# Retention, low-rank mixer and two feed-forwards on one core: the head of a token block is fetched back from DRAM when its turn comes

## The chip, the cores and the metric

The kernel runs on one core of one Trainium2 chip. The metric is device time in microseconds (us) of one execution; less is better. Engines are named as in the profile: PE (TensorE matmuls), PEld (TensorE weight loads), DVE (VectorE), ACT (ScalarE), POOL (GpSimd), and SP, whose queue (SPq) issues every DMA of this kernel in the order in which they are written.

## The reference

Three layers on 8 sequences of 576 tokens, model width 512:

```
ret = (scale * q k^T) * Dmat            # decaying causal weights, 8 heads of 64
x   = ret @ v                           # [8, 576, 512]
u   = x + (x^T U V)^T                   # rank 32, over the 576 tokens of a sequence
x2  = u + relu(u @ w_ch1) @ w_ch2       # 512 -> 2048 -> 512
k   = relu(mix_k(x2) @ w_k); v = (k*k) @ w_v
out = sigmoid(mix_r(x2) @ w_r) * v      # mix: each token with the one before it
```

Everything is fp32; a product is made of three fp32r matmuls from a high and a low part of each operand (high x high, low weight x high, high weight x low).

## The kernel before

The 4608 tokens are cut in two ways that do not fit each other: 8 batches (sequences) of S = 576 and 9 blocks of BT = 512. Block b consists of the last 64b columns of batch b-1 and the first 512-64b columns of batch b. I call the former the **head** of block b.

**The first stage** runs over 40 steps, five to a batch (`step_of`, i = 5b+p). A step does the retention of 128 tokens of its batch (lines 839 to 967: `scores`, `decay`, `inter`, `own`, `gain`, `states`, `leave`), and between those PE is filled with `hidden(n)`: n of the 16 products of block b-1 with `w_ch1` (12 matmuls each, line 383; ACT applies the ReLU out of one of two PSUM banks, line 389, and SP stores the result, line 394). So while batch b is in its five steps, PE works off the hidden products of block b-1. After the last step of batch b come `low_rank_sum` (two steps later) and `later` (three steps later), which puts eight `mix` matmuls and then `mix_store(b)` on the list `todo`; one entry of it is taken after each third of a hidden product.

**mix_store(b)** writes batch b's u to DRAM (`u_blk[b]` and the head of `u_blk[b+1]`), splits its first columns into the high and low parts of block b, and splits the rest at once into the head of block b+1. The parts of a block are four SBUF units (`ublk[t]`: `uh` x2, `ul` x2, [128, 2, 512] each). The block's hidden products read them through the whole of the next batch, so from `mix_store(b)` on, eight units are held: four of block b in use, and four of block b+1 with only the head in them.

**The pool.** All of this is in the pool `big`, 35 units of 4 KB per partition, one tag. A unit goes to the next tile in the program's order and its new writer waits by a semaphore for the last reader of the old tile. Besides `ublk` and 16 units of resident `w_ch1`, `big` holds the q/k/v loads (`qk`, `kv`, loaded four steps ahead) and, between the hidden products, the **weight conversions**: `slot()` takes a weight that is stored as float64 through a raw load (`wkraw`, `wv_raw`, `wsraw`, `wrraw`), ACT's word arithmetic (lines 100, 104), DVE's join (107), ACT's cast of a high part (lines 132, 270, 314) and POOL's or DVE's low part (lines 133, 271, 315), and stores it to DRAM (`keys`, `gates`, `second`, `wv_kept`, `first`). The order of every engine is the order written here (a manual schedule); nothing overtakes.

After the first stage (to about 546 us) come the pair of last blocks in seven products (line 1342), the down projection (line 557), and the gates, keys and values (lines 1429, 1525).

Of the kernel before, what the change touches and what calls it, by code (L numbers as in the profile page):

```python
# [9 lines left out]
F32 = mybir.dt.float32  # L10
F32R = mybir.dt.float32r
# [5 lines left out]
ALU = mybir.AluOpType  # L17
PSUM = bass.MemoryType.PSUM

B, H, S, D = 8, 8, 576, 64  # L20
# [10 lines left out]
L = 64  # L31
# [7 lines left out]
PAIR = (NB - 2, NB - 1)  # L39
# [4 lines left out]
def retention_mixer_kernel(ctx: ExitStack, tc: tile.TileContext, io):  # L44
    nc = tc.nc

    consts = ctx.enter_context(tc.tile_pool(name="consts", bufs=1))
    big = ctx.enter_context(tc.tile_pool(name="big", bufs=35))
# [3 lines left out]
    u_blk = [dram.tile([128, KD, BT], F32, name=f"ub{t}") for t in range(NB)]  # L52
# [7 lines left out]
    def unit(pool, dt, nm):  # L60
        return pool.tile([128, 2, 512], dt, tag="unit", name=nm)
# [6 lines left out]
    def bank(n, nm):  # L68
        return psum[-1].tile([128, 512], F32, tag=f"b{n}", name=nm, bufs=1)
# [4 lines left out]
    def turn(kind, banks, nm):  # L74
        i = turns.get(kind, 0)
        turns[kind] = i + 1
        return bank(banks[i % len(banks)], nm)
# [211 lines left out]
    def first_sums(g):  # L289
        got = {}  # L290

        def whole():
            got["x"] = [cv.tile([128, 512], F32, tag="cf", name="cf", bufs=5) for _ in range(2)]
            for i, x in enumerate(got["x"]):
                f = g + HF * i
                w, c = w1[f // 4], slice((f % 4) * 128, (f % 4 + 1) * 128)
                for k in range(2):
                    nc.vector.tensor_tensor(
                        x[:, 256 * k:256 * k + 256].rearrange("p (k n) -> p k n", n=128),
                        w.h[k][:, :, c].bitcast(F32), w.l[k][:, :, c].bitcast(F32), op=ALU.add,  # L300
                    )

        def sums():
            x, y = got["x"]
            a11, a12, a21, a22 = x[:, :256], x[:, 256:], y[:, :256], y[:, 256:]
            nc.vector.tensor_tensor(a22, a21, a22, op=ALU.add)
            nc.vector.tensor_tensor(a21, a11, a21, op=ALU.subtract)
            nc.vector.tensor_tensor(a11, a22, a11, op=ALU.subtract)
            nc.vector.tensor_tensor(a12, a12, a11, op=ALU.subtract)

        def part(i):
            x = got["x"][1 - i]
            y = got[i] = unit(big, F32R, f"fs{g}_{i}")
            nc.scalar.copy(y[:, 0], x)  # L314
            nc.vector.tensor_tensor(y[:, 1], x, y[:, 0].bitcast(F32), op=ALU.subtract)  # L315

        def store(i):
            nc.sync.dma_start(
                kept_1[g][:, i], got[i].bitcast(F32).rearrange("p l (s n) -> p l s n", n=256)
            )  # L320

        return [whole, sums, lambda: part(0), lambda: store(0), lambda: part(1), lambda: store(1)]
# [35 lines left out]
    ublk = {}  # L358


    def split_u(t, c0, x, n):
        if t not in ublk:
            ublk[t] = (
                [unit(big, F32R, f"uh{t}_{j}") for j in range(2)],
                [unit(big, F32R, f"ul{t}_{j}") for j in range(2)],
            )
        h, l = ublk[t]
        for j in range(2):
            hj, xj = h[j][:, :, c0:c0 + n], x[:, 2 * j:2 * j + 2]
            nc.scalar.copy(hj, xj)  # L370
            nc.vector.tensor_tensor(l[j][:, :, c0:c0 + n], xj, hj.bitcast(F32), op=ALU.subtract)
# [398 lines left out]
    with ExitStack() as st:  # L770
# [27 lines left out]
        def scale_k(b, p):  # L798
            n = 2 if p < NC - 1 else 1
            k = kv[b, p][:, :n, :256].rearrange("p c (h d) -> p c h d", d=D)  # L800
            nc.gpsimd.tensor_tensor(k, k, ktab[:, p, :n].to_broadcast([128, n, NP, D]), op=ALU.mult)  # L801
# [223 lines left out]
        def mix(b, k, s):  # L1025
            o, n = SEG[s]
            ps = turn("m", ("n", 0, 1), f"mx{b}_{k}_{s}") if b == 0 else bank("n", f"mx{b}_{k}_{s}")
            nc.tensor.matmul(  # L1028
                ps[:, :n], gst[b][:, k * 128:(k + 1) * 128], vst[:, o:o + n], start=True, stop=True
            )  # L1030
            u = xt[b][:, k, o:o + n]
            nc.vector.tensor_tensor(u, ps[:, :n], u, op=ALU.add)  # L1032

        def mix_store(b):
            o = (b + 1) * BT - b * S
            u = xt.pop(b)
            if b < PAIR[0]:
                split_u(b, BT - o, u[:, :, :o], o)
            if b + 1 < PAIR[0]:
                split_u(b + 1, 0, u[:, :, o:], S - o)  # L1040
            nc.sync.dma_start(u_blk[b][:, :, BT - o:], u[:, :, :o])
            nc.sync.dma_start(u_blk[b + 1][:, :, :S - o], u[:, :, o:])
            if b < PAIR[0]:
                ready.extend((b, f) for f in range(NF))
            if b + 1 == PAIR[0]:
                for j in range(2):
                    even.append(unit(big, F32, f"ue{j}"))
                    nc.sync.dma_start(even[j][:, :, :S - o], u_blk[b + 1][:, 2 * j:2 * j + 2, :S - o])
            if b == PAIR[0]:
                for j in range(2):  # L1050
                    nc.gpsimd.tensor_copy(even[j][:, :, BT - o:], u[:, 2 * j:2 * j + 2, :o])
                    odd.append(u[:, 2 * j:2 * j + 2, o:])


        todo, ready = [], []
        even, odd = [], []

        def mixes(n):
            for _ in range(n):
                if todo:  # L1060
                    todo.pop(0)()

        def later(b):
            for k in range(KD):
                for s in range(2):
                    todo.append(lambda k=k, s=s: mix(b, k, s))
            todo.append(lambda: mix_store(b))

        def hidden(n, convert=True):
# [75 lines left out]
        def stages(i):  # L1145
            for stage in early.pop(i, []):
                stage()
# [22 lines left out]
        for g in range(HF):  # L1170
            x = first_sums(g)
            if sums:
                before, begin = sums[-1], x[0]
                sums[-1] = lambda before=before, begin=begin: (before(), begin())
                x = x[1:]
            sums.extend(x)

        def load_to(n):
            while units and N - len(units) < n:
                load(*units.pop(0))  # L1180
# [17 lines left out]
        def next_qtab(p):  # L1198
            for a in range(NP):
                nc.scalar.activation(  # L1200
                    qtab[:, p, a], qtab[:, p - 1, a], AF.Copy, scale=step[:, a, 0:1]
                )
# [5 lines left out]
        def plan(i, fn, *args, where=due):  # L1208
            where.setdefault(i, []).append((fn, args))
# [3 lines left out]
        def products_of(i):  # L1213
            inter(i)
            own(i)
            if i + 1 < N:
                scores(i + 1)
                gain(i + 1)

        def leaves_of(i):  # L1220
            if i + 1 < N:
                decay(i + 1)
            from_state(i)
            if i + 1 < N:
                states(i + 1)
            leave(i)

        def step_of(i):
            b, p = seq[i]
            load_to(i + 4)  # L1230
            if i + 2 < N:
                scale_k(*seq[i + 2])
            for fn, args in first.pop(i, []):
                fn(*args)
            products_of(i)
            if i == NC:
                mixes(9)
            leaves_of(i)
            last = p == NC - 1
            if last and b == 0:  # L1240
                plan(i, natural, b, p)
                plan(i + 1, low_rank, b, p, where=first)
                plan(i + 1, low_rank_sum, b, where=first)
                plan(i + 1, later, b, where=first)
            else:
                plan(i + 1, natural, b, p)
                plan(i + (1 if i == NC - 2 else 2), low_rank, b, p)
                if last:
                    plan(i + 2, low_rank_sum, b)
                    plan(i + 3, later, b)  # L1250
            if i < NC - 1:
                next_qtab(i + 1)
            for fn, args in due.pop(i, []):
                fn(*args)
            if not ready:
                mixes(9)
            n = FIRST[i - NC] if i < len(FIRST) + NC else FULL[p] if b < B - 1 else LAST[p]
            for x in range(2):
                if b:
                    hidden((n + 1 - x) // 2, False)  # L1260
                if i or x:
                    stages(2 * i + x)
                if i > 2 * NC + 2 and not todo:
                    quiet.append(i)
                    slot(new=len(quiet) % 2 == 1 or len(quiet) > 40)
                    if sums:
                        sums.pop(0)()

        for i in range(N):
            step_of(i)  # L1270
# [12 lines left out]
        while ready:  # L1283
            if len(ready) == 3:
                load_first(0)
            t, f = ready.pop(0)
# [393 lines left out]
```

## Time and profile before

| | |
|---|---|
| median of 3 runs | 1443.59 us (1439.63 to 1444.34) |
| the profiled execution | 1441.68 us, span of its instructions 1439.9 us |
| TensorE clock granted, mean of the span | 0.970 |
| PE / DVE / ACT / POOL busy | 94% / 64% / 47% / 26% of the span |

A granted clock of 1.00 is 2.4 GHz, its other level, 0.5, is 1.2 GHz; a stretch in which both occur shows a mean between. Times in the trace count from the first instruction.

### The profile page before, as it was taken

How to read it: one execution, taken by the hardware profiler on the slowest of the kernel's cores; microseconds unless marked ns; L12 is line 12 of the kernel's file. 1: busy time of each engine (PE TensorE's matmuls, PEld its weight loads, DVE VectorE, ACT ScalarE, POOL GpSimd, SP SyncE). 2: the span in 40 equal slices, each digit the busy share in tenths (PEclk: the TensorE clock that was granted, in tenths of full speed). 3: DMA queues.
4: the chain of work that ended last, by engine and by line, in shares of the span. 5: the costliest groups of instructions: out<-in, count | busy, mean ns of one | idle time of the engine just before them, and what ended most of it. 6: DMA issues, size and time to landing. Idle time of an engine off the chain costs nothing.

```text
span 1439.9 us, 26131 instructions
## 1 busy us (share of the span) xinstructions
PE 1350.4 (94%) x10248; PEld 1103.1 (77%) x10248; DVE 915.8 (64%) x1268; ACT 677.3 (47%) x1185; POOL 379.8 (26%) x317
## 2 busy tenths in 40 slices
PE   7899885788869989999999999999999999999998
PEld 5688674667657778778888888888888888888897
DVE  3644442455335243577979798788797797687753
ACT  4654433244344345654444444466455455565431
POOL 2341232243415101402222121220411402303312
PEclk8899998999989999999999999999999999999999
DMA  9667586689849628799978888589238157075272
GB/s 346 223 228 256 196 301 222 216 289 313 296 158 357 236 107 263 263 372 408 323 255 287 278 281 278 206 294 342 96 147 284 38 214 254 1 254 184 72 279 89
DMA packets 134827, 342.11 MB, mean 238 GB/s; under 512 B 16432, under 2 KB 29616, under 8 KB 134704
## 3 DMA queue, kind: packets, MB, share of 16 engines
q1 hardware_dynamic: 134704, 340.44, 67.2%
q8 instruction: 81, 1.33, 0.4%
q14 instruction: 42, 0.34, 0.1%
HBM read 232.38 MB, written 108.00 MB: 236 GB/s over the span
## 4 chain that ended last, share of the span: by engine, by line
PE 70%; DMA 5%; DVE 4%; ACT 2%; issue 2%; SPq 1%; POOL 1%; DVEq 0%; ACTq 0%; POOLq 0%
PE v L1525 13%; PE h L383 11%; PE gc L557 6%; PE ga L557 6%; PE gd L557 6%; PE kd L1429 3%; PE kc L1429 3%; PE ka L1429 3%; PE gb L557 3%; PE kb L1429 2%; PE rd L1429 2%; PE rc L1429 2%; PE ra L1429 2%; PE c L639 1%; PE c L638 1%
## 5 line engine op out<-in xcount | busy, mean ns | idle before, releaser
L389 ACT ACTIVATE hs<-h 128x512 f32<-128x512 f32 x112 | 65.8, 596 | 155.0 <-PE h L383 153.3
L1481 POOL TENSOR_TENSOR vl<-m,vh 128x512 fp32r<-128x512 f32 (+1 forms) x40 | 47.7, 1193 | 310.2 <-ACT vh L1480 238.8
L516 ACT CAST sbh<-rb 128x1024 fp32r<-128x1024 f32 x64 | 67.3, 1052 | 52.0 <-PE gd L557 41.0
L1525 PE MATMUL v<-vh,wv_0u 128*128 128x512 f32 x288 | 88.7, 389 | 0.0
L1525 PE MATMUL v<-vh,wv_1u 128*128 128x512 f32 x288 | 88.7, 389 | 0.0
L517 DVE TENSOR_TENSOR sbl<-rb,sbh 128x1024 fp32r<-128x1024 f32 x64 | 84.3, 1317 | 3.4 <-ACT sbh L516 3.3
L516 ACT CAST sah<-ra 128x1024 fp32r<-128x1024 f32 (+1 forms) x64 | 53.5, 837 | 57.7 <-DVE ra L498 29.4
L517 DVE TENSOR_TENSOR sal<-ra,sah 128x1024 fp32r<-128x1024 f32 (+1 forms) x64 | 66.6, 1040 | 20.3 <-PE gd L557 12.2
L315 DVE TENSOR_TENSOR fs<-cf,fs 128x512 fp32r<-128x512 f32 x16 | 12.3, 767 | 103.3 <-ACT fs L314 92.2
L1481 POOL TENSOR_TENSOR vl<-c,vh 128x512 fp32r<-128x512 f32 (+1 forms) x40 | 62.2, 1575 | 25.8 <-ACT vh L1480 25.8
L1032 DVE TENSOR_TENSOR xt<-mx,xt 128x256 f32<-128x256 f32 x64 | 28.7, 456 | 56.8 <-PE mx L1028 56.7
L1525 PEld LDWEIGHTS v<-vh,wv_1u 128*128 128x128 f32 x288 | 54.1, 188 | 11.2
L1525 PEld LDWEIGHTS v<-vh,wv_0u 128*128 128x128 f32 x288 | 53.9, 188 | 11.0
L383 PE MATMUL h<-uh,w_2h 128*128 128x512 f32 x112 | 35.2, 440 | 27.9 <-ACT hs L389 27.9
L1480 ACT CAST vh<-m 128x512 fp32r<-128x512 f32 (+1 forms) x40 | 23.2, 580 | 75.3 <-DVE m L1479 75.3
L801 POOL TENSOR_TENSOR kv<-kv,ktab 128x512 f32<-128x512 f32 (+1 forms) x40 | 40.7, 1018 | 63.8 <-DMA kv<-in_kv 57.6
L1525 PE MATMUL v<-vl,wv_0u 128*128 128x512 f32 x144 | 56.0, 389 | 0.0
L1525 PE MATMUL v<-vl,wv_1u 128*128 128x512 f32 x144 | 56.0, 389 | 0.0
L601 POOL TENSOR_TENSOR x<-x,ur 128x512 f32<-128x512 f32 x16 | 25.1, 1581 | 105.7 <-DVE x L597 101.7
L670 ACT ACTIVATE tp<-x2l,omu 128x511 f32<-128x511 f32 x72 | 50.9, 712 | 3.1 <-DMA x2l<-xb 3.1
L853 DVE TENSOR_TENSOR pm<-up,dtab 128x512 f32<-128x512 f32 (+1 forms) x40 | 25.3, 632 | 41.1 <-PE up L839 41.1
L574 POOL TENSOR_TENSOR m<-m,ur 128x512 f32<-128x512 f32 x8 | 12.3, 1559 | 139.2 <-ACT m L571 139.2
(375 smaller groups left out, 3999.3 us busy)
## 6 DMA issues: line engine op xcount, KB each, us to landing
wk<-keys SPq DMA_DIRECT2D x80, 512.0 KB, 6.0
rb<-hp SPq DMA_DIRECT2D x64, 512.0 KB, 6.5
hp<-hs SPq DMA_DIRECT2D x112, 256.0 KB, 3.8
wr<-gates SPq DMA_DIRECT2D x40, 512.0 KB, 6.1
qk<-in_qk SPq DMA_DIRECT2D x32, 512.0 KB, 6.0
kv<-in_kv SPq DMA_DIRECT2D x32, 512.0 KB, 6.3
ra<-hp SPq DMA_DIRECT2D x32, 512.0 KB, 7.1
ur<-ub SPq DMA_DIRECT2D x18, 512.0 KB, 6.4
```

The lines of the kernel that those rows point to most:

```text
L383: nc.tensor.matmul(hps[t, f], w.part(lo, k, fo), u[k // 2][:, k % 2, :], start=(part == 0 and k == 0), stop=(part == 2 and k == KD - 1),)
L389: nc.scalar.activation(h, hps.pop((t, f)), AF.Relu)
L516: nc.scalar.copy(hi_, src)
L517: nc.vector.tensor_tensor(lo_, src, hi_.bitcast(F32), op=ALU.subtract)
L557: nc.tensor.matmul(group[g][p], l[:, col(p)], r, start=(h == 0 and j == 0 and i == 0), stop=(i == 2 and last), skip_group_check=True,)
L670: nc.scalar.activation(tp[:, 1:], x[:, :BT - 1], AF.Copy, scale=omu[:, j, k:k + 1])
L801: nc.gpsimd.tensor_tensor(k, k, ktab[:, p, :n].to_broadcast([128, n, NP, D]), op=ALU.mult)
L853: nc.vector.tensor_tensor(m[:, :, :n], t[:, :, 0:n * 128].rearrange("p g (x i) -> p g x i", i=2 * L), dtab.to_broadcast([128, 2, n, 2 * L] ...
L1032: nc.vector.tensor_tensor(u, ps[:, :n], u, op=ALU.add)
L1429: nc.tensor.matmul(ps[b], l, r[:, i], start=(part == 0 and i == 0 and j == 0), stop=(i == 1 and j == 2), skip_group_check=True,)
L1481: eng.tensor_tensor(l, x, h.bitcast(F32), op=ALU.subtract)
L1525: nc.tensor.matmul(vacc[t][o], w.part(lo, g, col(o)), x[:, i, :], start=(g == 0 and i == 0 and j == 0), stop=(g == NG - 1 and i == 1 and j ...
```

## The change

`mix_store(b)` no longer splits the head of block b+1 (but for b = 0). In its place `fetch_head(b)`, two steps after batch b's last one, allocates two units `uf` and loads block b's head from `u_blk[b]` by two DMAs; `split_head(b)`, put on `todo` just ahead of `mix_store(b)`, allocates the four units of `ublk[b]` and splits the head into them (ACT copy, DVE subtract). It is done for b = 2 to 6. The two `mixes(9)` become `mixes(10)`, since the list has one entry more.

```
+        def fetch_head(b):
+            heads[b] = [unit(big, F32, f"uf{b}_{j}") for j in range(2)]
+            for j, x in enumerate(heads[b]):
+                nc.sync.dma_start(x[:, :, :L * b], u_blk[b][:, 2 * j:2 * j + 2, :L * b])
+
+        def split_head(b):
+            ublk[b] = tuple([unit(big, F32R, f"u{x}{b}_{j}") for j in range(2)] for x in "hl")
+            for j, x in enumerate(heads.pop(b)):
+                hj, xj = ublk[b][0][j][:, :, :L * b], x[:, :, :L * b]
+                nc.scalar.copy(hj, xj)
+                nc.vector.tensor_tensor(ublk[b][1][j][:, :, :L * b], xj, hj.bitcast(F32), op=ALU.subtract)
...
         def mix_store(b):
...
-            if b + 1 < PAIR[0]:
-                split_u(b + 1, 0, u[:, :, o:], S - o)
+            if b == 0:
+                split_u(1, 0, u[:, :, o:], S - o)
...
+            if 1 < b < PAIR[0]:
+                todo.append(lambda: split_head(b))
             todo.append(lambda: mix_store(b))
...
                     plan(i + 2, low_rank_sum, b)
+                    if 1 < b < PAIR[0]:
+                        plan(i + 2, fetch_head, b)
                     plan(i + 3, later, b)
```

(`L` is 64.) On PE and POOL no instruction moves. On SP the two loads of a head stand behind the batch's last q/k/v load and ahead of the next store of a hidden product (`hp<-hs`); `ub` are the blocks in DRAM. Of before, in the middle of batch 1's hidden products:

```order
L792 DMA qk_4_2277<-in_qk 128x512
L794 DMA kv_4_2279<-in_kv 128x512
L394 DMA hp_75<-hs_9_2390 128x512
L394 DMA hp_75<-hs_10_2406 128x512
L184 DMA wv_raw_2422<-in_moe_w_v 128x512
```

and of the change:

```order
L792 DMA qk_4_2269<-in_qk 128x512
L794 DMA kv_4_2271<-in_kv 128x512
L1039 DMA uf_0_2362<-ub_68 128x2x128
L1039 DMA uf_1_2363<-ub_68 128x2x128
L394 DMA hp_75<-hs_9_2386 128x512
L394 DMA hp_75<-hs_10_2402 128x512
L184 DMA wv_raw_2418<-in_moe_w_v 128x512
```

Two DMAs came in; nothing else moved. On ACT, at the end of the same hidden products (`hs_14` and `hs_15` are the last two), the copies of before that prepare blocks 2 and 3:

```order
L389 ACTIVATE hs_14_2618<-h_14_2599 128x512
L370 CAST uh_0_1845<-xt_1495 128x2x384
L370 CAST uh_1_1846<-xt_1495 128x2x384
L370 CAST uh_0_2625<-xt_1495 128x2x192
L370 CAST uh_1_2626<-xt_1495 128x2x192
L389 ACTIVATE hs_15_2648<-h_15_2635 128x512
```

and of the change, which prepares block 2 alone, its head from `uf`:

```order
L389 ACTIVATE hs_14_2614<-h_14_2595 128x512
L1045 CAST uh_0_2617<-uf_0_2362 128x2x128
L1045 CAST uh_1_2618<-uf_1_2363 128x2x128
L370 CAST uh_0_2617<-xt_1495 128x2x384
L370 CAST uh_1_2618<-xt_1495 128x2x384
L389 ACTIVATE hs_15_2644<-h_15_2625 128x512
```

Four copies stay four, and DVE's subtractions change alike. What moves most is not an instruction but the units: every tile of `big` behind the first change lies elsewhere. On ACT, with the semaphores that a row waits for (DMAHWn: a DMA's landing, or an engine's name), in the conversion of `wkf` 3 in the middle of block 2's hidden products, before:

```order
L389 ACTIVATE hs_8_3108<-h_8_3095 128x512 [waits PE_49]
L270 CAST wkh_0_3111<-wkf_2812 128x512 [waits DMAHW2_49,PE_49]
L270 CAST wkh_0_3111<-wkf_2812 128x512
L100 ACTIVATE ca<-wkraw_0_2960 128x512 [waits DMAHW0_49]
L104 ACTIVATE wkf_3117<-wkraw_0_2960 128x512 [waits Pool_49]
L100 ACTIVATE ca<-wkraw_1_2962 128x512 [waits DMAHW1_49]
L104 ACTIVATE wkf_3117<-wkraw_1_2962 128x512
L314 CAST fs_1_3126<-cf 128x512 [waits DMAHW1_49,DMAHW0_49]
```

and of the change:

```order
L389 ACTIVATE hs_8_3104<-h_8_3091 128x512 [waits DMAHW0_49,PE_49]
L270 CAST wkh_0_3107<-wkf_2808 128x512 [waits DMAHW5_49,DMAHW4_49]
L270 CAST wkh_0_3107<-wkf_2808 128x512
L100 ACTIVATE ca<-wkraw_0_2956 128x512 [waits DMAHW2_49]
L104 ACTIVATE wkf_3113<-wkraw_0_2956 128x512 [waits DMAHW1_49]
L100 ACTIVATE ca<-wkraw_1_2958 128x512 [waits DMAHW3_49,Activation_49]
L104 ACTIVATE wkf_3113<-wkraw_1_2958 128x512
L314 CAST fs_1_3122<-cf 128x512 [waits PE_49]
```

The writer of `wkf` waited for POOL (the last reader of the tile that had its unit); it now waits for the landing of a store (of `wv_kept`). Counted in the two built programs, between the first ReLU of one block and that of the next, the tiles of `big` that are newly placed, how many of the 35 units are then in use on average, and how many of the new tiles take a unit whose old tile had its last reader after the tile placed just before:

| block whose products PE works off | in use, before | at once, before | in use, changed | at once, changed |
|---|---|---|---|---|
| 1 | 32.6 | 3 of 31 | 29.8 | 0 of 33 |
| 2 | 33.7 | 14 of 37 | 31.1 | 1 of 39 |
| 3 | 33.0 | 2 of 40 | 30.2 | 0 of 42 |
| 4 | 34.1 | 18 of 36 | 31.6 | 4 of 38 |
| 5 | 32.3 | 6 of 23 | 28.8 | 0 of 29 |

## Rows read from the trace of the kernel before

**Rows 1.** The page: TensorE clock granted in 40 slices of 36 us, in tenths.
```profile
PEclk8899998999989999999999999999999999999999
```

**Rows 2.** Stretches from each block's first ReLU to the next's: blocks 1 to 5.
```profile
core 0: us, PE busy (x) PEld busy (x) DVE busy (x) ACT busy (x) POOL busy (x), PEclk, DMA share, GB/s
...
120.10:186.20 66.10, 61.46 (x805) 49.52 (x804) 32.94 (x59) 28.38 (x53) 16.55 (x15) 0.95 0.73 244
186.20:278.70 92.50, 66.88 (x806) 52.54 (x805) 34.49 (x63) 31.08 (x59) 29.39 (x29) 0.87 0.68 240
278.70:353.60 74.90, 64.47 (x805) 51.14 (x805) 35.60 (x56) 33.46 (x65) 29.08 (x26) 0.93 0.85 289
353.60:435.20 81.60, 64.23 (x805) 51.00 (x804) 30.13 (x57) 32.18 (x60) 26.24 (x26) 0.90 0.69 242
435.20:497.30 62.10, 60.66 (x850) 49.02 (x850) 25.20 (x49) 24.67 (x49) 24.53 (x23) 1.00 0.89 315
```

**Rows 3.** Who PE waited for, 186 to 436 us: us, times, longest.
```profile
PE h L383 <- ACT hs L389: 28.5, 7, 9.0
PE mx L1028 <- DVE xt L1032: 9.8, 3, 6.7
PE mx L1028 <- ACT xs L987: 8.8, 2, 8.1
PE up L872 <- ACT w L936: 3.1, 1, 3.1
PE up L872 <- DVE y L950: 2.5, 1, 2.5
```

**Rows 4.** Who ACT waited for, 186 to 436 us.
```profile
ACT wkf L104 <- POOL wkl L271: 14.3, 2, 8.9
ACT wsf L104 <- POOL wsl L271: 13.6, 2, 7.5
...
ACT fs L314 <- PE up L872: 7.8, 2, 5.3
...
ACT ca L100 <- DMA wv_raw<-in_moe_w_v: 3.8, 1, 3.8
```

**Rows 5.** Timeline, POOL, ACT and PE around 240 us (idle before a row in brackets).
```profile
236.54 2.48 POOL L271 TENSOR_TENSOR wkl<-wkf,wkh 128x512 fp32r<-128x512 f32 x2 [15.98 <-DMA keys<-wkh]
...
239.06 0.66 ACT L104 ACTIVATE wkf<-wkraw 128x512 uint32<-128x512 uint8 x1 [8.87 <-POOL wkl L271]
...
244.74 0.79 PE L383 MATMUL h<-uh,w_2h 128*128 128x512 f32 x1 [8.99 <-ACT hs L389]
```

**Rows 6.** Timeline, ACT and PE, 249 to 262 us.
```profile
249.84 0.62 ACT L132 CAST wv_0p<-cf 128x512 fp32r<-128x512 f32 x1 [4.67 <-PE up L872]
...
261.81 0.64 PE L1028 MATMUL mx<-vst,gt 96*128 96x320 f32 x1 [6.75 <-DVE xt L1032]
```

**Rows 7.** Timeline, ACT and POOL, 403 to 416 us.
```profile
403.95 1.14 ACT L270 CAST wsh<-wsf 128x512 fp32r<-128x512 f32 x2 [0.53 <-PE dn L891]
...
411.76 0.66 ACT L104 ACTIVATE wsf<-wsraw 128x512 uint32<-128x512 uint8 x1 [6.10 <-POOL wsl L271]
...
409.25 2.48 POOL L271 TENSOR_TENSOR wsl<-wsf,wsh 128x512 fp32r<-128x512 f32 x2 [6.87 <-DMA second<-wsh]
```

**Rows 8.** Stretches with a busy DMA; columns as in Rows 2.
```profile
325.00:375.00 50.00, 46.53 (x617) 37.55 (x618) 26.58 (x47) 22.63 (x42) 19.02 (x19) 0.97 0.90 307
...
450.00:480.00 30.00, 30.00 (x500) 24.47 (x499) 13.29 (x26) 13.63 (x27) 18.70 (x18) 1.00 1.00 359
```

**Rows 9.** DMA issues: KB each, median us to landing; then timeline, SPq and ACT.
```profile
ur<-ub SPq DMA_DIRECT2D x18, 512.0 KB, 6.4
...
472.56 0.56 SPq L794 DMA_DIRECT2D kv<-in_kv  x1
...
482.88 0.70 ACT L370 CAST uh<-xt 128x256 fp32r<-128x256 f32 x2
```

**Rows 10.** Who SP's queue waited for, 186 to 436 us.
```profile
SPq L794 <- PE h L383: 14.7, 1, 14.7
```

More of the change, by code (lines that the diff above doesn't have):

```diff
@@ L1032, in mix @@
             nc.vector.tensor_tensor(u, ps[:, :n], u, op=ALU.add)
+        heads = {}
+        def fetch_head(b):
[8 more added lines that the diff above has]
+                nc.vector.tensor_tensor(ublk[b][1][j][:, :, :L * b], xj, hj.bitcast(F32), op=ALU.subtract)
         def mix_store(b):
@@ L1236, in step_of @@
             if i == NC:
-                mixes(9)
+                mixes(10)
             leaves_of(i)
@@ L1255, in step_of @@
             if not ready:
-                mixes(9)
+                mixes(10)
             n = FIRST[i - NC] if i < len(FIRST) + NC else FULL[p] if b < B - 1 else LAST[p]
```

## The prediction

> **What bounds the kernel now.** The profiled execution took 1441.7 us, 1.8 us more than its span and 1.9 us less than the median shown; the sum below is made against 1441.7, and so is the forecast. About 0.3% (4.3 us) is what a measurement of this kernel can tell from no change.
>
> I read the slices of the page first. The granted clock is below 9 tenths at the start and in four slices between 140 and 470 us, and never behind them [rows 1]: what the first stage loses is lost there. The change edits that stage alone, so I cut it into stretches from each block's first ReLU to the next's [rows 2]. Each holds the same work (192 hidden matmuls, five retention steps, eight mixes), and five lengths come out of it: 66.1, 92.5, 74.9, 81.6 and 62.1 us. The reader is to see that the last has PE busy for 60.66 us at clock 1.00, with 1.44 us idle, while the three in the middle idle for 25.6, 10.4 and 17.4 us and are also busy longer (66.9, 64.5, 64.2) at a mean clock of 0.87 to 0.93. So 60.7 us is what PE needs, and blocks 1 to 4 lose 66.1 + 92.5 + 74.9 + 81.6 - 4 x 60.7 = 72.3 us, 58.0 of it idle and 14.3 at the lower clock, 1.2 GHz, which sets in where PE has idled.
>
> Then the waits of PE in 186 to 436 us: 28.5 us for the ReLUs of ACT that free a PSUM bank, 9.8 for DVE and 8.8 for ACT ahead of a mix, 3.1 for ACT's state copy [rows 3]. ACT is busy for 31 to 33 us in each of these stretches [rows 2], so it is not short of time; it stands. The view of its own waits says for what: 14.3 and 13.6 us for POOL's low parts, 7.8 us for matmuls of the retention [rows 4]. None of these is data that ACT needs. `wkf` is made of a raw load, `fs` of sums of DVE; they wait for the last reader of the tile whose unit they get. One such wait in full, at 240 us [rows 5]: POOL's `wkl` waits until 236.5 for a store (of `keys`) that still reads its unit, 15.98 us of idle time; ACT's `wkf`, whose unit is the one that this `wkl` reads last, waits behind it for 8.87; behind `wkf` on ACT stand the conversion's other rows, the copies `gs` and `gt`, and the ReLU for which PE idles 8.99 us. The table of units says the same without times: where 14 of 37 and 18 of 36 new tiles take a unit that was in use a moment ago (blocks 2 and 4), PE idles for 25.6 and 17.4 us, where it is 2 or 3 (blocks 1 and 3) for 4.6 and 10.4.
>
> **The change part by part.**
>
> *Four units free for most of a batch.* In use go from 33.0-34.1 to 30.2-31.6 of 35, and units that are taken at once from 34 to 5 in blocks 2 to 4. In the changed program the `wkl` of the case at 240 us gets the unit of the conversion's `wkl` before it, and its `wkf` that of a `wv` part, both stored long since. I went through PE's waits in 186 to 436 us and asked of each whether ACT's wait behind it is gone:
> - The 28.5 us for ReLUs are seven waits. Behind five (25.1 us) stand `wkf`, `wv`, `fs`, `wsf` and `wrh` tiles that now get units free for long: gone. Two (3.4 us) hang on DVE's and ACT's chain of states; I keep them.
> - The 9.8 us: the longest, 6.75, begins with `wv_0p` waiting 4.67 us on ACT [rows 6]; then follow POOL's low part and DVE's sums, up to the mix at 261.81. Only the 4.67 goes, 2.1 us stay. Of the other two (3.1 us), 2.2 begin at a 4.3 us wait of `fs`: gone. Saved 6.9.
> - The 8.8 us: 8.1 hang on `wsf`, which still gets the unit that POOL's `wsl` reads last. `wsl` itself need no longer wait for its store and can start when ACT's `wsh` is done (405.1), not at 409.25 [rows 7]: I take 4.2 us as saved.
> - The 3.1 us (behind `wkf` again) and a 2.5 us one that ends on DVE, behind an `fs`: gone, 5.6 [rows 3].
>
> Together 41.8 of 53.4 us. Block 1's 4.6 us: ACT waits 1.6 for POOL and 1.4 for a raw load that SP held back for a unit; 3.0 saved. Block 5's 1.44 is a wait of a `wsh` for its unit: gone. **Idle saved: 46.2 of 59.4 us.** The slow clock's 14.3 us follow the idle time: x 46.2/59.4 = **11.1 us**. Bounds of both: nothing, if other waits replace them, and all 73.7.
>
> *Two DMAs more per block, b = 2 to 6.* 64b columns x 512 rows x 4 bytes = 131 KB x b, 2.6 MB in all, at the 359 GB/s of a full stretch [rows 8] 7.3 us of DMA time, beside PE. No row shows these loads, but the later ones from the same tensor land in 6.4 us [rows 9]. The copy needs the head eight mixes after the issue. The shortest such distance is block 6's: its last `kv` load is issued at 472.6 and `uh` is copied at 482.9 [rows 9], so the head has some 9 us for 6.4; for block 2 it is nearly 30. Price 0; without this cover, up to 3 us once. In SP's queue the issues add 10 x 0.5 us; behind them stand stores that have their tiles for several us.
>
> *The copies.* Four ACT copies and four DVE subtractions a block stay as many and go on the same engines; the columns change by at most 64. Price 0. The list is one entry longer, so `mix_store` comes a third of a hidden product (0.9 us of PE work) later and the split of the block with it; the products of the next block are behind a step's retention matmuls in PE's order, so 0.
>
> *What the compressed stage asks of the DMA.* Blocks 2 to 4 move 92.5 x 0.240 + 74.9 x 0.289 + 81.6 x 0.242 = 63.6 MB, and their DMA share times length is 62.9 + 63.7 + 56.3 = 182.9 us [rows 2]; with 1.6 MB of heads 187.3. After the savings above these stretches would last 249 - 41.8 - 10.6 = 197 us: a share of 0.95. At 0.90 PE idled 3.47 of 50 us, at 1.00 none in 30 [rows 8], so the give-back lies between 0 and 197/50 x 3.47 = 14 us, and I take 10, nearer to the mixed stretch.
>
> The Trainium skill, "DMA: Bandwidth & Descriptors", section Specifications, puts the HBM limit of a core at about 358 GB/s; by it 65.2 MB need 182 us, an estimate from that page, which would forbid more than the pace of block 5 but not the sum here. The 359 GB/s stretch agrees with it.
>
> **Sum:** 46.2 + 11.1 - 10 = 47.3 us; 1441.7 - 47.3 = 1394.4, rounded 1394. Stages behind 546 us keep their order and their waits; 0.
>
> **The rivals.**
> - *All comes back.* If an ACT that never stands also shortens the chains of DVE that I kept, blocks 1 to 4 run at block 5's pace: 315.1 - 4 x 62.1 = 66.7 us, 1375. For it: block 5 does the same work with a DMA share of 0.89. Against: blocks 2 and 3 convert more, and `wsf` still waits.
> - *The DMA becomes the bound.* The loads of raw weights, q/k/v and heads then land late, and ACT waits for a `ca` row where it now waits for a unit (it did for 3.8 us [rows 4]). If the three stretches take 215 us in place of 197, the gain is 57.3 - 28 = 29, at 1413. For it: a share of 0.95 in a queue whose order is fixed; against: 30 us at 1.00 with PE never idle.
> - *Slower: the head comes late.* If SP reaches the fetch so late that `split_head` waits, ACT stands with the ReLU and the mixes behind it, at each of five boundaries. SP's longest wait is 14.7 us [rows 10]; where the distance is 9 to 30 us the copy would wait some 10 us at worst, and only above 10 us a boundary (50 us) does the kernel lose; with 13 us each, 1459.
> - *No change.* The waits could be of the conversion itself, whose order is fixed: ACT, POOL, DVE in turn. Then ACT waits as long for the data as for the units, 1442. Against: `wsl` had its data (`wsh`) 4 us before it ran [rows 7].
>
> **How the numbers follow.** Forecast 0.60, its own range 1384 to 1404. All comes back 0.12; DMA bound 0.20; no change 0.04; slower 0.04. The forecast, half of "all comes back" and most of the DMA case make 0.8: **1374 to 1414**. Faster 0.60 + 0.12 + 0.20 = 0.92, within 0.3% 0.04, slower 0.04.
>
> **What would show it.** Right: the waits of `wkf` on POOL and of `wv`, `fs`, `wrh` on stores and on `up` gone from ACT's list; blocks 2 to 4 at 63 to 68 us each with the clock at 0.95 or more; `wsf` still waiting once for POOL; a DMA share of 0.9 or above; no ACT wait for `uf`. Wrong: stretches unchanged, or ACT waiting for `ca` rows' loads, or `uh` for `uf<-ub`. The prediction fails most easily if the waits that I kept as chains are shorter or longer than 13 us, or if the DMA gives back more than 14.

## The result and the profile after

The median went from 1443.96 us (four runs, 1439.63 to 1446.4) to 1387.98 us (four runs, 1383.92 to 1390.9): a ratio of 0.9613 with an interval of 0.9579 to 0.9648, 56 us faster in the medians. The profiled executions differ by less, 1441.7 to 1390.9 us, 50.8 us, and the sums below are made against that pair. The forecast was 1394 us, within 1374 to 1414.

The page's slices of the granted clock, where [rows 1] had two slices below 9 tenths behind the two at the start (216 to 252 and 396 to 432 us; the prediction counts four):

```profile
PEclk8899999999999999999999999999999999999999
```

Neither is left. The stretches from each block's first ReLU to the next's, in the columns of [rows 2], blocks 1 to 5:

```profile
121.20:186.10 64.90, 61.26 (x805) 49.59 (x804) 32.49 (x60) 28.12 (x53) 16.59 (x15) 0.95 0.75 252
186.10:251.40 65.30, 61.19 (x805) 49.27 (x804) 33.72 (x60) 31.03 (x60) 28.79 (x29) 0.95 0.94 347
251.40:318.60 67.20, 62.05 (x805) 49.72 (x804) 37.17 (x56) 33.50 (x64) 29.40 (x26) 0.95 0.94 331
318.60:384.40 65.80, 61.22 (x806) 49.44 (x805) 31.93 (x57) 31.81 (x60) 27.66 (x26) 0.95 0.92 334
384.40:446.50 62.10, 60.51 (x850) 48.99 (x850) 27.72 (x50) 26.35 (x51) 24.61 (x23) 1.00 0.88 302
```

Blocks 2 to 4 took 92.5, 74.9 and 81.6 us and now take 65.3, 67.2 and 65.8. Their idle time (length less PE's busy time) fell from 53.4 to 13.8 us, the clock rose to 0.95 and the DMA share to 0.92 to 0.94. The busy time of the other engines in these stretches is nearly what it was (ACT 96.3 us for 96.7, DVE 102.8 for 100.2, POOL 85.9 for 84.7). Over the five blocks the length fell from 377.2 to 325.3 us, by 51.9; block 1 begins 1.1 us later than before, which leaves the 50.8.

What PE waits for in 186 to 385 us (us, times, longest), all rows of the answer, to be held against [rows 3]:

```profile
PE mx L1028 <- DVE xt L1032: 8.8, 3, 4.1
PE mx L1028 <- ACT xs L987: 2.9, 1, 2.9
PE h L383 <- ACT hs L389: 2.1, 1, 2.1
```

And ACT in the same stretch, to be held against [rows 4]:

```profile
ACT hs L389 <- PE h L383: 72.7, 33, 7.9
ACT xt L966 <- DVE w L938: 8.2, 1, 8.2
ACT ca L100 <- DMA wv_raw<-in_moe_w_v: 8.2, 5, 2.7
...
ACT wsf L104 <- POOL wsl L271: 1.5, 1, 1.5
```

The 28.5 us for ReLUs are 2.1. ACT's waits for units, 14.3 us of `wkf`, 13.6 of `wsf` and 7.8 of `fs`, are gone but for 1.5. Its waits for late raw loads (`ca`) have grown from 3.8 us to 8.2, in five waits of at most 2.7. ACT still stands, but its largest row is now the ReLU's wait for PE's matmuls: it is early, and idle time of an engine that is not the bottleneck costs nothing. The one row that hardly shrank is the first of PE's, the mixes behind DVE: 9.8 us before, 8.8 now.

The head's own view, `uf` (median duration of each operation, what its engines waited for, landing times):

```profile
L1039 SPq DMA_DIRECT2D uf<-ub x10: 377/453/1517, 151.8 to 418.5; - x10
...
its engine sat idle before it (us, times) until:
  ACT uh L1045: 6.9, 6
...
DMA to landing us min/median/max: 4.5/5.6/7.7
```

No copy waits for a landing. The 6.9 us are DVE's subtractions waiting for ACT's copies.

### The profile page after: what moved, and what is told of

It reads as the page before. It is cut to its first block, busy times and chain, and to the rows that moved or that the text cites. A ratio compares the mean times of both kernels' runs of the same rounds, so it can differ in the third digit from the quotient of the medians.

```text
span 1389.0 us, 26137 instructions
## 1 busy us (share of the span) xinstructions
PE 1340.4 (97%) x10248; PEld 1099.0 (79%) x10248; DVE 920.1 (66%) x1268; ACT 677.8 (49%) x1185; POOL 380.9 (27%) x317
## 4 chain that ended last, share of the span: by engine, by line
PE 84%; DMA 7%; DVE 5%; ACT 2%; issue 1%; POOL 1%; SPq 0%; DVEq 0%; ACTq 0%; POOLq 0%
PE h L383 19%; PE v L1543 14%; PE gc L557 6%; PE ga L557 6%; PE gd L557 6%; PE kc L1447 4%; PE kd L1447 4%; PE ka L1447 4%; PE gb L557 3%; PE kb L1447 2%; PE rd L1447 2%; PE rc L1447 2%; PE ra L1447 2%; PE xn L977 1%; PE fa L1360 1%
## 5 line engine op out<-in xcount | busy, mean ns | idle before, releaser
L517 DVE TENSOR_TENSOR sal<-ra,sah 128x1024 fp32r<-128x1024 f32 (+1 forms) x64 | 66.5, 1038 | 18.6 <-PE gd L557 10.4
L1032 DVE TENSOR_TENSOR xt<-mx,xt 128x256 f32<-128x256 f32 x64 | 28.8, 457 | 62.1 <-PE mx L1028 62.1
L1543 PEld LDWEIGHTS v<-vh,wv_0u 128*128 128x128 f32 x288 | 53.9, 188 | 11.1
L315 DVE TENSOR_TENSOR fs<-cf,fs 128x512 fp32r<-128x512 f32 x16 | 13.8, 865 | 67.2 <-ACT fs L314 67.2
L1497 DVE SCALAR_TENSOR_TENSOR m<-m 128x512 f32<-128x512 f32 (+1 forms) x40 | 44.8, 1119 | 1.4
```

The source lines that it names most:

```text
L517: nc.vector.tensor_tensor(lo_, src, hi_.bitcast(F32), op=ALU.subtract)
L1497: nc.vector.scalar_tensor_tensor(x, x, 0.0, x, op0=ALU.max, op1=ALU.mult)
L1543: nc.tensor.matmul(vacc[t][o], w.part(lo, g, col(o)), x[:, i, :], start=(g == 0 and i == 0 and j == 0), stop=(g == NG - 1 and i == 1 and j ...
```

## The experiments

My theory, **A**: the engines stood for units of `big` that had been taken a moment after their last use, and the gain is that four units are no longer held through a batch. The rival, **B**: the gain is in something else that the change does (the head's split made later, the list one entry longer, the order on SP). On the size there were two further rivals: that the DMA, near its full share, takes back some of the gain, and that a chain of DVE holds what is left.

The base of some kernels is **inplace**, which needs no `uf`: the head lands in the units of the block's own low part and is split there. (Its expectation was written behind those of inplace_held4 and inplace_held2 below; "the same" is their way to fetch the head.)

```
-            heads[b] = [unit(big, F32, f"uf{b}_{j}") for j in range(2)]
+            heads[b] = [unit(big, F32R, f"ul{b}_{j}") for j in range(2)]
...
-            ublk[b] = tuple([unit(big, F32R, f"u{x}{b}_{j}") for j in range(2)] for x in "hl")
+            ublk[b] = [unit(big, F32R, f"uh{b}_{j}") for j in range(2)], heads.pop(b)
```

> The same, nothing held early: the low-part units when the head is fetched, the high parts when it is split, no uf units at all. Theory A: as the changed kernel or a little less, 1380 to 1391, since the changed kernel has few waits for units left. Theory B: the same.

Measured: 1386.31 us (1382.98 to 1387.64), ratio 0.9618 (0.9585 to 0.9652). It is the same as the change within the measurement; the two `uf` units make no difference that can be seen.

**The units alone.** inplace_held4 is inplace with the four units of block b+1 allocated where before allocated them, in `mix_store(b)`, and touched there with a one-column write, so that they are held through the batch; the fetch, the late split and the longer list stay.

```
+        def hold(b):
+            ublk[b] = tuple([unit(big, F32R, f"u{x}{b}_{j}") for j in range(2)] for x in "hl")
+            for x in (*ublk[b][0], *ublk[b][1]):
+                nc.vector.tensor_copy(x[:, 0, 0:1], omu[:, 0, 0:1])
...
+            if 0 < b < PAIR[0] - 1:
+                hold(b + 1)
```

> The head is fetched as in the changed kernel, but straight into the block's two low-part units, and all four units of the block are allocated in the mix_store one batch earlier, as the kernel before does: 34.0 and 33.7 units in use in blocks 4 and 2, 16 and 15 new tiles that take a unit at once, the counts of before. Theory A (units that come free too late): the gain is gone, 1430 to 1450 us, with the three middle blocks at 75 to 93 us each. Theory B (the gain comes from the work that left the batch's end and from its new place, whatever the units): as the changed kernel, 1384 to 1396.

Measured: 1446.15 us (ten runs, 1441.72 to 1449.34), ratio 1.0022 (1.0004 to 1.0041). The whole gain is gone. Its stretches of blocks 2 to 4, in the columns of [rows 2]:

```profile
187.20:279.60 92.40, 66.89 (x805) 52.58 (x804) 32.67 (x64) 30.90 (x59) 29.49 (x29) 0.87 0.69 245
279.60:354.60 75.00, 64.46 (x805) 51.12 (x805) 35.59 (x60) 33.41 (x65) 29.05 (x26) 0.93 0.86 293
354.60:440.00 85.40, 65.20 (x805) 51.50 (x804) 30.54 (x66) 31.92 (x60) 26.51 (x26) 0.86 0.70 242
```

and ACT's waits in 187 to 440 us:

```profile
ACT wsf L104 <- POOL wsl L271: 16.5, 2, 8.5
ACT wkf L104 <- POOL wkl L271: 14.1, 2, 8.8
```

They are the stretches of before to within 0.1 us in blocks 2 and 3 (block 4 is 3.8 us longer), and the waits of [rows 4] by name and nearly by size (that of `fs` is 7.8 us again). Everything that the change does, but for the units, is in this kernel; theory B falls.

**Half of the units.** inplace_held2 holds only the two `ul` units early.

> The same, with only the two low-part units allocated a batch earlier and the two high parts when the head is split: 32.3 and 32.7 units in use in blocks 2 and 4, 1 and 5 taken at once. Theory A: what counts is whether a unit is taken at once, so nearly all of the gain stays, 1386 to 1405. Theory B: 1384 to 1396. If the gain goes evenly with the units held, half of it: about 1415.

Measured: 1392.76 us (1384.78 to 1394.62), ratio 0.9649 (0.9610 to 0.9689). Counted in the built programs as in the table of the change, with the idle time of PE from each trace:

| kernel | in use, blocks 2 and 4 | at once, blocks 2 and 4 | PE idle, blocks 2 and 4, us |
|---|---|---|---|
| before | 33.7, 34.1 | 14, 18 | 25.6, 17.4 |
| inplace_held4 | 33.7, 34.0 | 15, 16 | 25.5, 20.2 |
| inplace_held2 | 32.3, 32.7 | 1, 5 | 7.5, 4.7 |
| the change | 31.1, 31.6 | 1, 4 | 4.1, 4.6 |
| inplace | 30.9, 31.5 | 1, 4 | 4.6, 3.7 |

The first two units freed bring nearly all. The idle time goes with the tiles that take a unit at once, not in step with the units in use. The counts fall into two groups (1 to 5, and 14 to 18), so what lies between them is not measured; and the count does not say all: block 3 before idles 10.4 us with 2 such tiles.

**The transfers.** Three kernels ask what the heads' loads cost. In noload nothing is loaded: POOL fills the head with zeros, so that 64b columns of u are left out of blocks 2 to 6.

```
-                nc.sync.dma_start(x[:, :, :L * b], u_blk[b][:, 2 * j:2 * j + 2, :L * b])
+                nc.gpsimd.memset(x[:, :, :L * b], 0.0)
```

> The changed kernel without the loads of the heads: GpSimd fills the head's columns with zeros, so 64b columns of u of blocks 2 to 6 are left out of the computation; all units, copies and subtractions stay. If the loads are hidden as predicted: 1384 to 1391, no different from the changed kernel. If they cost DMA or queue time: 1375 to 1383.

Measured: 1387.04 us (1386.94 to 1391.4), ratio 0.9616 (0.9592 to 0.964), with the change's 1387.98 inside. Taking the loads away gives nothing back, though POOL's fills are short (0.3 to 0.7 us each), so the loads were hidden; PE's wait for DVE ahead of the mixes stays at 7.7 us.

load2 fills the other columns of `uf` as well, which nothing reads: ten more DMAs, 2.6 MB more.

```
+                nc.sync.dma_start(x[:, :, L * b:], u_blk[0][:, 2 * j:2 * j + 2, L * b:])
```

> The changed kernel with the rest of the two uf units filled too, from block 0, which was stored long before: 10 DMAs and 2.6 MB more (7.3 us at 359 GB/s) that wait for no landing of their own unit. It separates bytes from queue: if blocks at a DMA share of 0.92 to 0.94 are bound by the DMA, 7 us or more are added, 1393 to 1402; if the loss of the threefold load came from SP standing for its own landings, 1385 to 1392.

Measured: 1386.07 us (1384.29 to 1389.2), ratio 0.9604 (0.958 to 0.9628): no loss. Its stretch of block 2 has a full DMA share, and is not longer than the change's:

```profile
186.00:250.00 64.00, 59.89 (x802) 48.13 (x801) 34.14 (x61) 31.00 (x59) 29.68 (x30) 0.97 1.00 359
```

load3 loads each head three times to the same place.

```
+                for _ in range(3):
+                    nc.sync.dma_start(x[:, :, :L * b], u_blk[b][:, 2 * j:2 * j + 2, :L * b])
```

> The changed kernel with every head loaded three times over into the same place: 5.2 MB and 20 DMAs more in the stage, some 14.6 us of DMA time in blocks that run at a share of 0.92 to 0.94. If the DMA is the bound of the compressed stage: 1398 to 1406. If it is not: within 5 us of the changed kernel, 1383 to 1395.

Measured: 1420.32 us (1415.32 to 1420.91), ratio 0.9844 (0.981 to 0.9877), 32 us over the change, outside both answers. SP's queue in 120 to 500 us waited for the loads' own landings:

```profile
SPq L1040 <- DMA uf<-ub: 61.9, 20, 6.5
```

ACT in the same stretch waited for what SP issued late:

```profile
ACT ca L100 <- DMA wv_raw<-in_moe_w_v: 25.0, 8, 11.7
...
ACT uh L1046 <- DMA uf<-ub: 8.2, 2, 7.2
```

and PE's largest row is the mixes behind ACT:

```profile
PE mx L1028 <- ACT xs L987: 14.6, 2, 12.3
```

The second and third load of a tile wait on SP until the one before has landed, 20 times, and the raw weights queued behind them come late for ACT (25.0 us where the change had 9.3). load3 adds twice load2's bytes and these waits at once, so it does not part the two by itself. Its rows show SP standing; where it lost most, in block 1 (75.7 us for the change's 64.9), the DMA's share in 160 to 200 us was 0.56, so the DMA was not short there; and load2's bytes by themselves have no price.

late asks how much room the fetch has. It is put on the list just ahead of the last two mixes, where it was issued two steps after the batch's last one.

```
+                todo.insert(len(todo) - 2, lambda: fetch_head(b))
...
-                    if 1 < b < PAIR[0]:
-                        plan(i + 2, fetch_head, b)
```

> The changed kernel with each head fetched two mixes ahead of its split in place of two steps after the batch's last one, so that some 2 us of PE work lie between issue and copy, where a head lands 4.5 to 7.7 us after its issue. If the copy must wait and ACT holds the ReLU behind it: ACT waits 3 to 5 us for uf at each of five boundaries (15 to 25 us), and PE, which has two banks of slack of about 2 us, loses 8 to 18 us with the lower clock: 1396 to 1406 us. If the boundary has more slack than that: within 4 us of the changed kernel, 1384 to 1392 us, ACT's wait for uf seen and PE not idle behind it.

Measured: 1385.67 us (1383.71 to 1388.31), ratio 0.9594 (0.9552 to 0.9636). From the view of `uf`:

```profile
  DMA uf<-ub: 3.4, 2
...
DMA to landing us min/median/max: 2.2/4.0/4.7
```

Two copies of ten waited, 1.7 us each, and the time shows no loss. The second answer held: the boundary has more room than the two mixes, and a head that is 1.7 us late costs nothing. In load3 two of these copies waited 5.4 and 5.9 us, there for stores (`gates` and `first`), and PE stood 2.7 and 3.4 us behind the block's copies: longer waits at this place are not free.

**The chain of DVE.** The mixes that PE still waits for stand behind rows like these. DVE's timeline in block 2 of the change (start, duration, instruction, idle before in brackets):

```profile
224.47 0.76 DVE L298 TENSOR_TENSOR cf<-w_2h,w_2l 128x256 f32<-128x256 f32 x2 [1.57 <-POOL wv_0p L133]
...
226.54 0.42 DVE L306 TENSOR_TENSOR cf<-cf 128x256 f32<-128x256 f32 x1
227.00 1.54 DVE L307 TENSOR_TENSOR cf<-cf 128x256 f32<-128x256 f32 x1
228.57 1.39 DVE L308 TENSOR_TENSOR cf<-cf 128x256 f32<-128x256 f32 x1
230.00 0.72 DVE L309 TENSOR_TENSOR cf<-cf 128x256 f32<-128x256 f32 x1
```

and PE's, one row, the mix that waits for DVE's addition of the mix before (233.22 to 233.63):

```profile
233.69 0.64 PE L1028 MATMUL mx<-vst,gt 96*128 96x320 f32 x1 [4.11 <-DVE xt L1032]
```

Four sums of `w_ch1` (lines 306 to 309) stand for 4.1 us (226.54 to 230.64) ahead of the retention's rows and of the mix's addition; neither reads them. Ahead of the sums stands the piece before them, line 298, which waits 1.57 us for POOL.

These pieces are taken from a list, in its order, at fixed places (p, x), step p of a batch and half x of a step; (1, 1) is the last place ahead of a batch's mixes. Which piece falls there differs: the four sums in block 2, line 298 in block 3, the cast `fs` with DVE's line 315 in blocks 1 and 4. inplace_sums2 is inplace with two pieces taken at (1, 0) and none at (1, 1). inplace_sums3 takes two at (0, 1) and none at (1, 1). Its expectation, below, says that one piece moves by a whole step; since the list keeps its order, what happens is that the pieces of (1, 0) and (1, 1) both move up by half a step. The edit of inplace_sums3:

```
-                    if sums:
+                    if sums and (p, x) != (1, 1):
+                        sums.pop(0)()
+                    if sums and (p, x) == (0, 1):
                         sums.pop(0)()
```

> The in-place version; besides, the piece of the sums of w_ch1 that DVE does in the last slot before a batch's mixes is done in the slot of half a step earlier, which gets two pieces. If what is left of PE's idle time (3.7 to 5.5 us a block) is the chain of DVE work ahead of the first mix add, 1372 to 1382; if it is ACT's wait for a late raw load, 1383 to 1389.

> The same piece moved to the second half of the batch's first step instead, a whole step earlier. Same two answers: 1372 to 1382 if it is DVE's chain, 1383 to 1389 if not.

Measured: inplace_sums2 1377.14 us (1376.37 to 1379.97), ratio 0.9545 (0.9522 to 0.9568); inplace_sums3 1372.78 us (1371.96 to 1375.31), ratio 0.9513 (0.949 to 0.9535), which is the fastest kernel here, 13.5 us below inplace. Its stretches of blocks 2 to 4, in the columns of [rows 2]:

```profile
182.00:242.70 60.70, 59.30 (x806) 47.65 (x806) 32.76 (x60) 31.03 (x60) 29.31 (x29) 1.00 1.02 370
242.70:306.00 63.30, 59.31 (x805) 47.52 (x804) 37.43 (x56) 33.22 (x65) 29.05 (x26) 1.00 0.99 354
306.00:369.80 63.80, 60.15 (x805) 48.90 (x804) 32.48 (x59) 31.66 (x60) 27.61 (x26) 0.97 0.94 345
```

and all that PE waits for in them:

```profile
PE mx L1028 <- ACT xs L987: 3.9, 2, 3.6
PE h L383 <- ACT hs L389: 3.9, 2, 2.0
PE mx L1028 <- DVE xt L1032: 1.1, 1, 1.1
```

The wait for DVE is 1.1 us where it was 8.8, and the DMA runs at its full share all through block 2 with PE idle for 1.4 us. What was left of PE's waits for DVE was the chain of pieces ahead of the mixes.

In block 2 it was not the four sums alone, as the two kernels show together. In both of them the sums have moved from (1, 1) to (1, 0) and take 1.7 to 1.8 us. In inplace_sums2 line 298 stands in the same place as before, waits longer for POOL, and the mix is as late as in inplace (4.2 us there):

```profile
218.71 0.76 DVE L298 TENSOR_TENSOR cf<-w_2h,w_2l 128x256 f32<-128x256 f32 x2 [3.23 <-POOL wv_0p L133]
...
227.63 0.63 PE L1028 MATMUL mx<-vst,gt 96*128 96x320 f32 x1 [4.31 <-DVE xt L1032]
```

In inplace_sums3 line 298 has moved up as well, waits for nothing, and the mix is 1.1 us late:

```profile
215.16 1.85 DVE L298 TENSOR_TENSOR cf<-w_2h,w_2l 128x256 f32<-128x256 f32 x2
...
227.06 0.41 PE L1028 MATMUL mx<-vst,gt 96*128 96x320 f32 x1 [1.15 <-DVE xt L1032]
```

Line 298 does not read what that POOL row writes. Its tile `cf` has one of five buffers of another pool, and in the built program of the change the last reader of that buffer is this POOL row; in inplace_sums3 the same piece gets a buffer that DVE itself read last. So it is again a wait for a buffer just released. The gain of inplace_sums2 lies elsewhere: block 1 takes 59.8 us in both kernels, 65.0 in inplace, and block 2 takes 66.4, 60.7 and 65.2.

before_sums3 makes the same edit in the kernel before, with nothing freed.

> The kernel before, nothing freed and no head fetched, with DVE's first-stage sum of w_ch1 moved from step 1 of each batch to step 0, as in inplace_sums3. Theory A (the units taken at once hold ACT up, and the DVE chain is a second, separate loss of some 10 to 13 us that shows only where ACT no longer stands): the units of blocks 2 and 4 are shifted but as full as before, so 1425 to 1450 us, at most 1% below before, with ACT still waiting for POOL's low parts by 10 us or more in 186 to 436 us. Rival (the DVE chain is what held the engines in the first place, and the freed units only moved it): most of the gain appears without the change, 1385 to 1410 us.

Measured: 1420.8 us (1417.24 to 1423.73), ratio 0.9837 (0.9798 to 0.9875), between the two answers: moving the pieces was worth 24 us here, not the 10 to 13 that I gave the chain. PE's two largest waits in 186 to 436 us:

```profile
PE h L383 <- ACT hs L389: 30.0, 9, 8.5
PE mx L1028 <- ACT xs L987: 4.3, 1, 4.3
```

and ACT's in the same stretch:

```profile
ACT wkf L104 <- POOL wkl L271: 13.8, 2, 8.4
ACT fs L314 <- PE up L872: 12.7, 3, 5.3
ACT wsf L104 <- POOL wsl L271: 9.8, 2, 7.4
```

The two losses come apart by name. Moving the pieces takes the wait for DVE ahead of the mixes away (9.8 us to none) and leaves the ReLU's at 30.0 (it was 28.5); freeing the units takes the ReLU's away and leaves DVE's at 8.8. The mixes' wait for ACT's `xs`, 8.8 us before, shrinks by either edit (4.3 and 2.9). The gains nearly add up: 1.6% by the pieces, 3.8% by the units in inplace, 4.9% by both.

## Why the prediction was right, and where it was not

**The mechanism was right.** That ACT stood for the units, not for data, and that PE's ReLU waits were the end of it, is what inplace_held4 shows: the units put back, all of it returns. The five ReLU waits that the forecast called gone (25.1 us of 28.5) are gone, and of the two that it kept (3.4 us) one of 2.1 us is there; the 5.6 us of state waits are gone, as forecast. Of `wsf`'s 8.1 us more went than the 4.2 that were taken: the row is 2.9 us. The blocks took 65 to 67 us, within the 63 to 68 that the prediction named as a sign of being right (which is its 197 us for three blocks without the 10 us that it gave back).

**Idle saved: 46.2 us in the sum, 40.4 measured** (59.4 us in blocks 1 to 5 before, 19.1 after). The term that was mis-sized is the one on the 9.8 us that PE waits for DVE: I said that 6.9 would go, since two of these waits begin with an ACT row that waited for a unit (the longer one in [rows 6]), and counted what ACT waited as saved. 1.0 us went. The ACT rows no longer wait, but DVE's own rows ahead of the mixes, with their wait for a `cf` buffer, are long enough by themselves: the wait in block 2 is 4.1 us where 2.1 were to stay, that in block 3 is 3.1 where none was, and that in block 4, behind ACT's `fs`, is 1.7 for 0.9. In block 3 a late raw load also stands in the chain: ACT waits 2.7 us for a `ca` row, a sign that the prediction had named as one of being wrong; what it adds there is not shown. These 5.9 us are as much as the whole error of the term; block 1 (1.0 saved for 3.0) and block 5 (nothing for 1.4) are offset by the ReLU's and `wsf`'s better results.

**Give-back of the DMA: 10 us in the sum, none that can be seen.** The stretches have the DMA share that the sum worked out (0.95 forecast, 0.92 to 0.94 measured), but bytes were not a price: with 2.6 MB less or more the time is the same, and inplace_sums3 runs block 2 at a share of 1.02. The 3.47 us of idle time in the 0.90 stretch [rows 8], from which I took 10, were not the DMA's: PE's waits there are one of 2.2 us for a ReLU and one of 2.2 for DVE ahead of a mix, both in [rows 3] and counted already. The stretch at 1.00 beside it, with none, was the row to go by. The rival in which the DMA becomes the bound falls with it.

**Slow clock: 11.1 us in the sum, 11.3 measured** (PE's busy time in blocks 1 to 4, 257.0 to 245.7). The size is right by luck, with a wrong base: the prediction says that each block holds the same work, but [rows 2] count 850 matmuls in block 5 and 805 in the others. inplace_sums3 has blocks 2 and 3 at clock 1.00 with 59.3 us of PE, so 60.7, taken from block 5, was too long for blocks 1 to 4, and the slow clock cost some 20 us before, not 14.3; some 8 of them are left in the change.

So 40.4 + 11.3 + 0.1 (block 5's busy time) - 1.1 (block 1 begins later) = 50.7 us measured, where the sum had 46.2 + 11.1 - 10 = 47.3: two terms too large, of opposite sign, which partly cancel. That the forecast is nearer than its terms is luck.

**The prices of nothing.** The loads of the head (noload), their distance to the copy (late) and the copies (inplace_held4 has the loads, their distance and the copies, and is 0.2% over before, with DVE's touching writes among it) cost nothing that can be measured, as forecast. For *Slower: the head comes late*, late shows that 1.7 us of waiting is free; the 10 us and more of that rival were not tried, and load3 shows that 5 to 6 us reach PE. SP standing is what cost in load3: 61.9 us in the queue and, with 5.2 MB more, 32 us of the kernel. *All comes back* asked that freed units shorten DVE's chain too; they don't, and its 1375 us needed the pieces moved as well (1372.78).

What stays open: before_sums3 gains 24.4 us between the profiled executions, where I had given the chain 10 to 13. Blocks 2 to 4 explain 18.0 of them (14.6 of idle time, nearly all at the mixes, and 3.4 of busy time at the slower clock), blocks 1 and 5 some 3; the 3 us behind block 5 are hardly more than four other kernels differ by there (939.8 to 942.5 us in the change, inplace, inplace_sums2 and inplace_sums3). Likewise the 1.1 us by which block 1 begins later in the change: six traces of kernels with the change's code up to there begin it between 119.2 and 122.2 us.

## What to carry to other kernels

Where an engine that is half idle still holds others up, ask of each of its waits whether it is for data or for the last reader of the tile whose buffer it gets; in a pool that rotates, count the tiles that take a buffer just released, since here two free buffers ended nearly all of the waits and two more brought little. A wait that ends in a chain goes only as far as the chain's own length: before calling it saved, add up the rows of the engine that stay in front, and their own waits for buffers. Before idle time in a stretch at a high DMA share is laid on the DMA, look whether another stretch at a higher share runs without a stall, as here, and what PE waits for by name.

## What the runs showed of the hardware

One core moved 370 GB/s for 60.7 us at a busy share of 1.02, with PE idle for 1.4 us in them (inplace_sums3). The prediction cited a limit of about 358 GB/s from the Trainium skill; "HBM Reference", section Specifications (TRN2), says that this is a core's share when both cores of a pair stream and that one alone gets well above it. The trace agrees with the latter, and the measurement decides: 358 GB/s is no bound for this kernel on one core. The trace of before had shown it too, behind the first stage, which the prediction passed over when it said that a stretch at 359 GB/s agrees with the limit:

```profile
650.00:675.00 25.00, 25.00 (x112) 20.71 (x111) 18.61 (x21) 12.12 (x16) 5.40 (x4) 1.00 1.03 410
```

Three DMAs in a row to the same place made SP wait 3.1 us on average for the landing of the one before (load3, 61.9 us in 20 waits); ten further DMAs to other columns of the same tiles (load2) show no such wait.

The same subtraction of DVE (line 307, 128x256) took 0.42 to 1.55 us in the eight times that it ran in the change. Four took 0.42, with no POOL row beside them; the other four (0.85 to 1.55) ran beside a POOL row for most of their time or all of it, the longest, at 227.00, beside one of line 271 that POOL did from 226.97 to 229.68. So these rows grew where POOL worked beside them; no kernel here moved POOL's row to try it.
